# An integer mask for a sine's argument, and batch 1's first stage begun two units sooner in a fused Fourier-mixing and maxout kernel

## The chip, the core and the metric

The kernel runs on one core of one Trainium2 chip. The metric is the device time of one execution in microseconds (us). Five queues matter: TensorE (PE, with its weight loads as PEld), VectorE (DVE), ScalarE (ACT), GpSimd (POOL, which also issues the loads of x and the scattered stores) and SyncE (SP, which only issues DMAs). Each works its instructions off in the order of the program.

## The reference

```python
def _attn_ref(x):                      # x: (8, 3072, 256)
    X = np.fft.fft(x, axis=1)
    X = np.fft.fft(X, axis=2)
    return X.real.astype(np.float32)

def _moe_ref(x, w1, w2, w3, w_out):    # x: (24576, 256), w: (256, 768), w_out: (768, 256)
    h = np.maximum(np.maximum(x @ w1, x @ w2), x @ w3)
    return h @ w_out
```

The output of the first, as 24576 rows of 256, is the input of the second.

## The kernel before

The Fourier transform along the 256 columns is folded into the weights: `md_all` and `nmd_all` hold a sine and its negative, of 256 columns each in two halves, and `product` multiplies them with the weights into `g_all` and, by `differ`, `gd_all`. The transform along the 3072 rows is made for each of the 8 batches by class `Mix` in two stages. Stage one is the pieces `s0` to `s6`: each multiplies up to eight of the 49 slabs of `xt` (one of two buffers, by the batch's parity) with the small table `tab` into PSUM, and an eviction copies that to `tb` (L403, L406, L412, L414). Stage two is the pieces `k`: matmuls of `yb` with the tables `te_tab` and `to_tab` (L464), evicted to `tE` and `tO`. Between the stages `tb` must become `yb`, transposed: for batch 0 by one DVE transpose (`t`, L432), for later batches through DRAM, by pieces `y` (`tb` to `db`, L421) and `z` (`db` to `yb`, L427), four DMAs each, on the SP queue. Piece `x` (`x0`) then writes one more column into `yb` (L453, L454, on ACT), so it waits for all four DMAs of `z`. Before stage one the upper half of `xt` must be filled with a mirrored copy of the lower (`mirror`, L134 and L138: on DVE for batch 0, on POOL or DVE for batch 1, on ACT afterwards).

The main loop has 18 units a batch (3 blocks of 512 tokens by 6 chunks of 128 hidden columns), 144 in all. A unit makes `pse` tiles on PE (`begin`; L488, L489, or L831, L832 for a split unit), and ACT and DVE take the maximum into `hp` (`unit_out`: ACT `stmp`, L501, then DVE, L502); then the unit before is finished with `gd_all` (`finish`, L495) and taken into `hm`. From unit 7 on every odd unit is split: the third weight goes ahead through `third` (PE L815 and L817, ACT `odd` L819, DVE `even` L820, POOL `plus` and `minus` L824), and DVE alone takes the maximum (L833, L845). Below, hp6 is the `hp` of unit 6, hm5 the `hm` of unit 5. The finished block is multiplied with `wout_bf` (L511, `l2_block`) over the following units, evicted by DVE (`ot`, L539), and stored by SP (L547) and POOL (L620).

What else is done in a unit is a plan by hand: `at(b, u, fn)`. The units 0 to 5 of batch 0 carry the rest of the preparation: `column` (psc, L354), `prep_second` (psw, L377, evicted to `gw` by DVE, L382, then ACT, L383). `ahead0` says which pieces of batch 1 go in which unit of batch 0:

```python
ahead0 = {5: ("s0", "s1"), 6: ("s2", "y0", "s3"), 7: ("s4", "s5", "s6", "y1", "u"),
          8: ("z0", "z1"), 12: ("x",), 13: ("kO0",), 14: ("v0", "kE0", "kO1"), ...
```

The pieces `s`, `k`, `e3`, `d3`, `pl`, `psc` and `psw` share the three PSUM banks of pool `ps_f`.

In the prologue (up to some 20 us) x of batch 0 comes in four chunks (`FIRST`), c0 to c3, of two loads each. DVE's order there is: small tables, `vm` (the argument of `md_all`'s sine), mirror c0, the reduction of `vm` by `_reduce` (L23, L25, L27), `wrap(0, 512)`, mirror c1, `wrap(512, 1024)`, mirror c2, mirror c3, three small ones for `sgn`, the eviction of s5 and the transpose. Matmuls named `warm` (L638) only keep PE busy.

Of the kernel before, what the change touches and what calls it, by code (L numbers as in the profile page):

```python
# [9 lines left out]
FP32 = mybir.dt.float32  # L10
BF16 = mybir.dt.bfloat16
INT32 = mybir.dt.int32
UINT32 = mybir.dt.uint32
AX = mybir.ActivationFunctionType
ALU = mybir.AluOpType
# [5 lines left out]
def _reduce(nc, w, v, q, period):  # L21

    nc.vector.tensor_scalar(out=q, in0=v, scalar1=1.0 / period, scalar2=ROUND,  # L23
                            op0=ALU.mult, op1=ALU.add)
    nc.vector.tensor_scalar(out=q, in0=q, scalar1=-ROUND, scalar2=-period,  # L25
                            op0=ALU.add, op1=ALU.mult)
    nc.vector.tensor_tensor(out=w, in0=v, in1=q, op=ALU.add)  # L27
# [24 lines left out]
def kernel(  # L52
# [9 lines left out]
    nc = tc.nc  # L62
# [38 lines left out]
    md_all = consts.tile([128, 512], BF16, tag="md_all")  # L101
    nmd_all = consts.tile([128, 512], BF16, tag="nmd_all")
# [26 lines left out]
    def mirror(b, s0, s1):  # L129

        t = xt[b % 2]
        fn = (nc.vector.tensor_copy, (nc.gpsimd.tensor_copy, nc.vector.tensor_copy)[s0 >= 25],
              nc.scalar.copy)[min(b, 2)]
        fn(out=t[64:128, s0:s1, 1:128], in_=t[0:64, s0:s1, 255:128:-1])  # L134
        if b < 2:
            if b == 0 and s0 < 40:
                fn = nc.scalar.copy
            fn(out=t[64:128, s0:s1, 0], in_=t[0:64, s0:s1, 128])  # L138
# [6 lines left out]
    gen = ctx.enter_context(tc.tile_pool(name="gen", bufs=1))  # L145
# [20 lines left out]
    kvec = gen.tile([128, NHALF + 1], FP32, tag="kvec")  # L166
# [38 lines left out]
    ang_o = gen.tile([128, NA], FP32, tag="ang_o")  # L205
    nc.vector.memset(ang_o, 0.0)
    rnd = gen.tile([128, 2], FP32, tag="rnd")
    nc.vector.memset(rnd[:, 0:1], ROUND)
    nc.vector.memset(rnd[:, 1:2], -ROUND)
    nc.vector.memset(ang_o[:, 15:32], 8.0)  # L210
# [2 lines left out]
    def small(name):  # L213
        return gen.tile([128, 1], FP32, name=name, tag=name)

    def scal(out, in0, s1, op0, s2=None, op1=None, eng=None):
        kw = {} if op1 is None else {"op1": op1}
        return (eng or nc.vector).tensor_scalar(out=out, in0=in0, scalar1=s1, scalar2=s2,
                                                op0=op0, **kw)

    def mad(out, in0, s1, in1):
        return nc.vector.scalar_tensor_tensor(out=out, in0=in0, scalar=s1, in1=in1,
                                              op0=ALU.mult, op1=ALU.add)
# [6 lines left out]
    phi, s_of = small("phi"), small("s_of")  # L230
# [8 lines left out]
    ang_q = gen.tile([128, NA], FP32, tag="ang_q")  # L239
    mad(ang_r, ang_r, alpha, ang_o)  # L240
    _reduce(nc, ang_r, ang_r, ang_q, 32.0)
    nc.scalar.activation(out=ang_q, in_=ang_r, func=AX.Sin, scale=float(2.0 * math.pi / 32.0))
    par = gen.tile([128, 2], FP32, tag="par")
    odd = gen.tile([128, 1], INT32, tag="odd")
    nc.vector.tensor_scalar(out=odd, in0=pidx_i, scalar1=1, scalar2=None, op0=ALU.bitwise_and)
    scal(par[:, 1:2], odd, 64.0, ALU.mult)
    scal(par[:, 0:1], odd, -64.0, ALU.mult, 64.0, ALU.add)
    nc.vector.tensor_copy(out=tab[:, 0:64:2], in_=ang_q[:, 0:32])
    scal(tab[:, 1:64:2], ang_q[:, 0:32], sig, ALU.mult)
    scal(tabx, ang_q[:, 32:NA], sgm, ALU.mult)  # L250

    dve = nc.vector.tensor_copy
    vm = gen.tile([128, 512], FP32, tag="vm")
    qm = gen.tile([128, 512], FP32, tag="qm")
    pf = gen.tile([128, 2], FP32, tag="pf")
    for fc in range(2):
        scal(pf[:, fc:fc + 1], pidx, float(128 * fc), ALU.add)
        for k, c in ((0, 64.0), (1, 0.0)):
            scal(vm[:, (2 * fc + k) * 128:(2 * fc + k + 1) * 128], dvec, pf[:, fc:fc + 1], ALU.mult,
                 c, ALU.add)  # L260

    q = gen.tile([128, NHALF + 1], FP32, tag="q")
    step = float(2.0 * math.pi / 3072.0)

    def phase(c0, c1):
        nc.scalar.activation(out=kvec[:, c0:c1], in_=kvec[:, c0:c1], func=AX.Identity,
                             scale=s_of, bias=phi)

    def turns(c0, c1):

        nc.scalar.activation(out=q[:, c0:c1], in_=kvec[:, c0:c1], func=AX.Identity,
                             scale=1.0 / 3072.0, bias=rnd[:, 0:1])
        nc.scalar.activation(out=q[:, c0:c1], in_=q[:, c0:c1], func=AX.Identity,
                             scale=1.0, bias=rnd[:, 1:2])

    def wrap(c0, c1):
        mad(kvec[:, c0:c1], q[:, c0:c1], -3072.0, kvec[:, c0:c1])

    phase(0, 512)
    turns(0, 512)  # L280
    phase(512, 1024)
    mirror(0, *FIRST[0])
    turns(512, 1024)
    _reduce(nc, vm, vm, qm, 256.0)
    nc.vector.tensor_copy(out=vm.rearrange("p (fc k c) -> p fc k c", fc=2, k=2)[:, :, :, 0],
                          in_=par.unsqueeze(1).to_broadcast([128, 2, 2]))
    wrap(0, 512)
# [360 lines left out]
    mirror(0, *FIRST[2])  # L648
    m.s(2, pool=ps_s)
    m.s(3, pool=ps_s)  # L650
    nc.scalar.activation(out=md_all, in_=vm, func=AX.Sin, scale=float(2.0 * math.pi / 256.0))
    warm_up(1)
    mirror(0, *FIRST[3])
    m.s(4, pool=ps_s)
# [2 lines left out]
    scal(sgn, sgn, 2.0, ALU.mult, -1.0, ALU.add)  # L657
    scal(dif, sgn, 1.0, ALU.subtract)
    m.s(5, pool=ps_s, evict=dve)
    m.s(6, pool=ps_s)  # L660
    m.t()
    warm_up(2)
    nc.scalar.activation(out=nmd_all, in_=vm, func=AX.Sin, scale=float(-2.0 * math.pi / 256.0))
    for k in range(3):
        load_w(k, 384, 768)
    m.u()
# [1 line left out]
    for (s0, s1) in HALVES:  # L668
        for h in range(2):
            load_x(1, s0, s1, h)  # L670
        if s0 == 0:
            nc.gpsimd.dma_start(out=wout_bf.rearrange("p (jc c) -> p jc c", jc=NJC),
                                in_=moe_w_out.rearrange("(jc p) c -> p jc c", jc=NJC))
# [59 lines left out]
    def at(b, unit, fn):  # L733
        plan.setdefault((b + unit // UNITS, unit % UNITS), []).append(fn)

    def piece(b, what):
        mm = mix(b)
        if what[0] == "s":
            mm.s(int(what[1:]), evict=dve if b == 1 and what in ("s3", "s5") else nc.scalar.copy)
        elif what[0] == "y":  # L740
            mm.y(*((0, 24), (24, NS))[int(what[1])])
        elif what[0] == "z":
            mm.z(int(what[1]))
        elif what[0] == "u":
# [12 lines left out]

    def fetch(b, k):
        half, h = divmod(k, 2)
        load_x(b, *HALVES[half], h)  # L760
# [14 lines left out]
        at(0, u, fn)  # L775

    for ch in range(4):
        at(0, (3, 3, 5, 5)[ch], lambda ch=ch: mirror(1, *CHUNKS[ch]))
        at(0, 4, lambda ch=ch: fetch(2, ch))
    for b in range(2, B):  # L780
        for ch in range(4):
# [2 lines left out]
        for ch in range(8):  # L784
            at(b - 2, 5 + ch + 3 * (b == 2), lambda b=b, ch=ch: turn(b, ch))
        at(b - 2, 13 + 3 * (b == 2), lambda b=b: mirror_first(b))

    ahead0 = {5: ("s0", "s1"), 6: ("s2", "y0", "s3"), 7: ("s4", "s5", "s6", "y1", "u"),
              8: ("z0", "z1"), 12: ("x",), 13: ("kO0",), 14: ("v0", "kE0", "kO1"),
              15: ("v1", "kE1"), 16: ("kO2",), 17: ("v2", "kE2", "end")}  # L790
    ahead = {1: ("s0", "s1"), 2: ("s2", "y0", "s3", "s6"), 3: ("s4", "s5", "y1", "u"),
             6: ("z0",), 7: ("z1",), 11: ("x",), 12: ("kO0",), 13: ("v0", "kE0", "kO1"),
# [1 line left out]
    for b in range(B - 1):  # L794
        for u, whats in (ahead0, ahead)[min(b, 1)].items():
            for what in whats:
                at(b, u, lambda b=b, what=what: piece(b + 1, what))
# [123 lines left out]
```

## Time and profile before

| what | value |
|---|---|
| median of 3 runs | 396.98 us (396.65 to 397.41) |
| profiled execution, its own time | 397.9 us |
| its span on the core | 396.1 us |
| PE, DVE, ACT, POOL busy | 96%, 80%, 67%, 84% of the span |
| q1 (DMAs of SP): packets, MB | 41978, 26.72 |
| q0 (DMAs of POOL): packets, MB | 24368, 26.53 |

The median and the profiled execution are executions of the same program; the span leaves out what lies before the first and behind the last instruction, 1.8 us here. Times in the rows of the profile count from the start of the span. In a row of the timeline the brackets say how long the engine had been idle before the instruction, and what ended that.

### The profile page before, as it was taken

What the parts mean: (1) busy time and instruction counts of PE and PEld (TensorE: products, weight loads), DVE (VectorE), ACT (ScalarE), POOL (GpSimd) and SP (SyncE); (2) the same over time, 40 slices, a digit from 0 to 9 for tenths busy, and PEclk for the clock granted to TensorE, in tenths of its full rate; (3) what the DMA queues carried; (4) which work ended last, traced back from release to release, by engine and by line L of the source; (5) the groups of instructions that cost most, each with busy time, mean ns of one, the idle gap of its engine ahead of it and who ended that gap; (6) DMA issues with size and microseconds to landing.
All of it is one profiled execution on the core that took longest, in us unless ns stands there. A gap on an engine that the chain in (4) does not pass through costs nothing.

```text
span 396.1 us, 8431 instructions
## 1 busy us (share of the span) xinstructions
PE 380.5 (96%) x2759; PEld 235.8 (60%) x2759; DVE 316.5 (80%) x528; ACT 263.7 (67%) x478; POOL 332.0 (84%) x432
## 2 busy tenths in 40 slices
PE   6699999999999999999999999999999999999994
PEld 2355555665665666656665666656665666666673
DVE  7986877787887988877887887877887887887982
ACT  5877669578867787578866788568866547545420
POOL 9994687879988899889988899889977898869993
PEclk9999999999999999999999999999999999999998
DMA  8999576494656876595666867395343553421234
GB/s 114 181 182 162 117 190 126 114 211 132 137 153 117 199 150 153 121 207 129 136 155 112 203 139 167 109 207 130 117 103 93 140 142 93 91 84 45 89 94 132
DMA packets 66901, 54.20 MB, mean 137 GB/s; under 512 B 32702, under 2 KB 62556, under 8 KB 66003
## 3 DMA queue, kind: packets, MB, share of 16 engines
q0 software_dynamic: 24368, 26.53, 35.2%
q1 hardware_dynamic: 41978, 26.72, 27.5%
q8 instruction: 21, 0.34, 0.4%
q10 hardware_dynamic: 512, 0.43, 0.4%
q14 instruction: 22, 0.18, 0.2%
HBM read 36.95 MB, written 30.81 MB: 171 GB/s over the span
## 4 chain that ended last, share of the span: by engine, by line
PE 88%; DMA 4%; DVE 2%; ACT 2%; POOL 1%; issue 1%; DVEq 0%; POOLq 0%; SPq 0%
PE po L511 30%; PE pse L495 12%; PE pse L488 8%; PE pse L489 8%; PE po L534 5%; PE pse L831 4%; PE pse L832 4%; PE e L815 4%; PE d L817 4%; PE ps L399 3%; PE ps L464 3%; PE pl L526 2%; DMA yb<-db 2%; DMA xt<-in_x_dram 2%; DVE yb L432 1%
## 5 line engine op out<-in xcount | busy, mean ns | idle before, releaser
L501 ACT ACTIVATE stmp<-pse 128x512 bf16<-128x512 f32 x150 | 89.5, 601 | 65.1 <-PE pse L495 41.4
L824 POOL TENSOR_TENSOR plus<-even,odd 128x512 bf16<-128x512 f32 x69 | 87.7, 1272 | 36.3 <-DVE even L820 28.5
L620 POOL DMA_INDIRECT out_dram<-ot,rows_m x92 | 102.4, 1113 | 17.9 <-issue 8.6
L824 POOL TENSOR_TENSOR minus<-even,odd 128x512 bf16<-128x512 f32 x69 | 87.5, 1268 | 0.0
L511 PE MATMUL po<-wout_bf,hp 128*128 128x256 bf16 x576 | 86.1, 273 | 0.0
L833 DVE SCALAR_TENSOR_TENSOR hp<-pse,plus 128x512 bf16<-128x512 f32 x69 | 47.6, 689 | 46.6 <-PE pse L832 27.1
L511 PE MATMUL po<-wout_bf,hm 128*128 128x256 bf16 x576 | 78.6, 273 | 0.0
L511 PEld LDWEIGHTS <-hp 128*128 128x128 bf16 x576 | 56.3, 98 | 26.1
L495 PE MATMUL pse<-tO,gd_all 128*128 128x512 bf16 x219 | 70.8, 379 | 0.0
L511 PEld LDWEIGHTS <-hm 128*128 128x128 bf16 x576 | 56.3, 98 | 16.4
L539 DVE TENSOR_TENSOR ot<-po,even 128x512 f32<-128x512 f32 x92 | 62.7, 681 | 0.0
L502 DVE TENSOR_TENSOR hm<-pse,stmp 128x512 bf16<-128x512 f32 x75 | 51.6, 688 | 9.4 <-ACT stmp L501 6.2
L502 DVE TENSOR_TENSOR hp<-pse,stmp 128x512 bf16<-128x512 f32 x75 | 51.3, 684 | 9.3 <-ACT stmp L501 8.0
L488 PE MATMUL pse<-tE,g_all 128*128 128x512 bf16 x150 | 56.8, 379 | 1.5 <-ACT stmp L501 0.7
L489 PE MATMUL pse<-tO,g_all 128*128 128x512 bf16 x150 | 56.8, 379 | 0.0
L820 DVE SCALAR_TENSOR_TENSOR even<-vb,wcol,e 128x512 f32<-128x512 bf16 x69 | 50.9, 737 | 0.0
L845 DVE SCALAR_TENSOR_TENSOR hm<-pse,minus 128x512 bf16<-128x512 f32 x69 | 47.0, 681 | 1.0 <-PE pse L489 0.5
L819 ACT ACTIVATE odd<-d 128x512 f32<-128x512 f32 x69 | 41.3, 599 | 6.0
L134 ACT COPY xt<-xt 64x762 bf16<-64x762 bf16 (+1 forms) x48 | 40.3, 839 | 1.1
L495 PEld LDWEIGHTS <-gd_all 128*128 128x128 bf16 x219 | 21.3, 97 | 23.0 <-issue 5.0
L534 PE MATMUL po<-gw,tO 128*128 128x512 bf16 x92 | 34.9, 380 | 0.0
L403 ACT CAST tb<-ps 128x512 bf16<-128x512 f32 x40 | 21.6, 588 | 14.8 <-PE ps L399 14.8
(175 smaller groups left out, 482.9 us busy)
## 6 DMA issues: line engine op xcount, KB each, us to landing
xt<-in_x_dram POOLq DMA_DIRECT2D x14, 384.0 KB, 8.7
out_dram<-ot SPq DMA_DIRECT2D x55, 96.0 KB
out_dram<-ot SPq DMA_DIRECT2D x64, 64.0 KB
db<-tb SPq DMA_DIRECT2D x21, 192.0 KB
vb<-vd SPq DMA_DIRECT2D x23, 128.0 KB
xt<-in_x_dram POOLq DMA_DIRECT2D x7, 400.0 KB, 6.7
xt<-in_x_dram POOLq DMA_DIRECT2D x7, 368.0 KB, 11.6
out_dram<-ot SPq DMA_DIRECT2D x62, 32.0 KB
```

Source lines behind the costliest of these rows:

```text
L488: nc.tensor.matmul(pse[:, 0:n], g_all[:, jc, 2 * i, :], te, start=True, stop=False)
L489: nc.tensor.matmul(pse[:, 0:n], g_all[:, jc, 2 * i + 1, :], to, start=False, stop=True)
L495: nc.tensor.matmul(pse, gd_all[:, jc, i, :], to, start=False, stop=True, skip_group_check=True)
L501: nc.scalar.activation(out=stmp[:, 0:n], in_=pses[0][:, 0:n], func=AX.Relu)
L502: nc.vector.tensor_tensor(out=dst, in0=src3, in1=stmp[:, 0:n], op=ALU.max)
L511: nc.tensor.matmul(po, hcols(jc), wout_bf[:, jc * 256:(jc + 1) * 256], start=False, stop=(jc == NJC - 1), skip_group_check=True)
L534: nc.tensor.matmul(po, to[:, cp], gw[:, 256:768], start=True, stop=True)
L539: nc.vector.tensor_tensor(out=ot.rearrange("p (h c) -> p h c", h=2), in0=po.rearrange("p (h c) -> p h c", h=2), in1=lin.unsqueeze(1).to_br ...
L620: stored(nc.gpsimd.indirect_dma_start(out, bass.IndirectOffsetOnAxis(ap=rows_m[0:128 - lo, at_row: at_row + 1], axis=0), ot[lo:128, 256:51 ...
L820: nc.vector.scalar_tensor_tensor(out=even3, in0=vb, scalar=wcol[:, jc:jc + 1], in1=e3, op0=ALU.mult, op1=ALU.add)
L824: nc.gpsimd.tensor_tensor(out=dst, in0=even3, in1=odd3, op=op)
L833: nc.vector.scalar_tensor_tensor(out=dst, in0=pse2, scalar=0.0, in1=sums[g][0], op0=ALU.max, op1=ALU.max)
```

## The change

The argument of the sine in `md_all` becomes an integer: `vm` and `par` are INT32 and offset by 128, one `bitwise_and` with 255 takes the place of the three operations of `_reduce`, and the two sines get a bias of minus and plus pi (`turn`). On ACT `phase(0, 512)` stands ahead of the small sine, and the sine to `md_all` stands behind the eviction of s4 and no longer ahead of it. Of batch 1, s0 and s1 go from unit 5 to 3, s2 and y0 from 6 to 4, s3 and s4 to 5, s5, s6, y1 and `u` to 6, z0 and z1 from 8 to 7; the mirrors on DVE of its second half go from unit 5 to 4. Its evictions s0, s1, s2 and s4 are on DVE (before: s3 and s5), the others on ACT. Later batches and the units from 8 on are as before.

```diff
+    turn = gen.tile([128, 2], FP32, tag="turn")
+    nc.vector.memset(turn[:, 0:1], -math.pi)
+    nc.vector.memset(turn[:, 1:2], math.pi)
...
+    def phase(c0, c1):
+        nc.scalar.activation(out=kvec[:, c0:c1], in_=kvec[:, c0:c1], func=AX.Identity,
+                             scale=s_of, bias=phi)
+
+    phase(0, 512)
     nc.scalar.activation(out=ang_q, in_=ang_r, func=AX.Sin, scale=float(2.0 * math.pi / 32.0))
-    par = gen.tile([128, 2], FP32, tag="par")
+    par = gen.tile([128, 2], INT32, tag="par")
...
-    scal(par[:, 1:2], odd, 64.0, ALU.mult)
-    scal(par[:, 0:1], odd, -64.0, ALU.mult, 64.0, ALU.add)
+    scal(par[:, 1:2], odd, 64.0, ALU.mult, 128.0, ALU.add)
+    scal(par[:, 0:1], odd, -64.0, ALU.mult, 192.0, ALU.add)
...
-    vm = gen.tile([128, 512], FP32, tag="vm")
-    qm = gen.tile([128, 512], FP32, tag="qm")
+    vm = gen.tile([128, 512], INT32, tag="vm")
...
-        for k, c in ((0, 64.0), (1, 0.0)):
+        for k, c in ((0, 192.0), (1, 128.0)):
...
-    phase(0, 512)
     turns(0, 512)
...
-    _reduce(nc, vm, vm, qm, 256.0)
+    nc.vector.tensor_scalar(out=vm, in0=vm, scalar1=255, scalar2=None, op0=ALU.bitwise_and)
...
-    nc.scalar.activation(out=md_all, in_=vm, func=AX.Sin, scale=float(2.0 * math.pi / 256.0))
     warm_up(1)
     mirror(0, *FIRST[3])
     m.s(4, pool=ps_s)
...
     m.s(5, pool=ps_s, evict=dve)
+    nc.scalar.activation(out=md_all, in_=vm, func=AX.Sin, scale=float(2.0 * math.pi / 256.0),
+                         bias=turn[:, 0:1])
     m.s(6, pool=ps_s)
     m.t()
     warm_up(2)
-    nc.scalar.activation(out=nmd_all, in_=vm, func=AX.Sin, scale=float(-2.0 * math.pi / 256.0))
+    nc.scalar.activation(out=nmd_all, in_=vm, func=AX.Sin, scale=float(-2.0 * math.pi / 256.0),
+                         bias=turn[:, 1:2])
...
-            mm.s(int(what[1:]), evict=dve if b == 1 and what in ("s3", "s5") else nc.scalar.copy)
+            mm.s(int(what[1:]), evict=dve if b == 1 and what in ("s0", "s1", "s2", "s4") else nc.scalar.copy)
...
-        at(0, (3, 3, 5, 5)[ch], lambda ch=ch: mirror(1, *CHUNKS[ch]))
+        at(0, (3, 3, 4, 4)[ch], lambda ch=ch: mirror(1, *CHUNKS[ch]))
...
-    ahead0 = {5: ("s0", "s1"), 6: ("s2", "y0", "s3"), 7: ("s4", "s5", "s6", "y1", "u"),
-              8: ("z0", "z1"), 12: ("x",), 13: ("kO0",), 14: ("v0", "kE0", "kO1"),
+    ahead0 = {3: ("s0", "s1"), 4: ("s2", "y0"), 5: ("s3", "s4"), 6: ("s5", "s6", "y1", "u"),
+              7: ("z0", "z1"), 12: ("x",), 13: ("kO0",), 14: ("v0", "kE0", "kO1"),
```

More of the change, by code (lines that the diff above doesn't have):

```diff
@@ L263 @@
     step = float(2.0 * math.pi / 3072.0)
-    def phase(c0, c1):
-        nc.scalar.activation(out=kvec[:, c0:c1], in_=kvec[:, c0:c1], func=AX.Identity,
-                             scale=s_of, bias=phi)
     def turns(c0, c1):
```

## The prediction

> **What bounds the kernel now.** I read the page first, then stretches of the span, then the chain of work that ended last, then the timelines of the stretches where PE idles. A change of 0.2% (0.8 us) is about what a measurement here can tell from none.
>
> ```profile
> PE 380.5 (96%) x2759; PEld 235.8 (60%) x2759; DVE 316.5 (80%) x528; ACT 263.7 (67%) x478; POOL 332.0 (84%) x432
> ```
>
> In the rows of the stretches stand the length, then busy us (and instructions) of PE, PEld, DVE, ACT and POOL, then PE's granted clock, the share of the DMA engines and GB/s.
>
> ```profile
> 20.00:37.35 17.35, 15.95 (x144) 9.30 (x141) 13.18 (x22) 13.21 (x30) 13.39 (x28) 1.00 1.11 172
> 37.35:45.36 8.01, 7.25 (x44) 3.71 (x43) 6.45 (x13) 5.88 (x12) 2.78 (x3) 1.00 0.72 132
> 45.36:59.83 14.47, 13.66 (x92) 8.59 (x91) 10.91 (x18) 9.81 (x18) 12.41 (x17) 1.00 0.68 166
> 59.83:65.00 5.17, 4.92 (x42) 3.00 (x43) 3.83 (x6) 5.07 (x9) 3.98 (x5) 1.00 0.87 150
> 65.00:380.00 315.00, 315.00 (x2280) 196.57 (x2279) 257.38 (x404) 214.37 (x383) 272.12 (x327) 1.00 0.58 133
> ```
>
> From 65 to 380 us PE is never idle at full clock: nothing in those 315 us can be gained, and what PE gains ahead of them reaches the end whole. The idle PE is 17.35-15.95 = 1.40, 0.76, 0.81 and 0.25 us in the four stretches ahead, 3.22 us together, and the prologue ahead of 20 us, which hangs on a chain and not on PE. The change works only there.
>
> ```profile
> 5.35 6.28 DMA xt<-in_x_dram
> ...
> 15.23 0.70 DVE tb L406
> 16.04 3.76 DVE yb L432
> ...
> 59.53 0.07 ACT yb L453
> ```
>
> The chain runs through the eviction of s5 into the transpose, and late in batch 0 it leaves PE for ACT's L453, which waits for `yb` from DRAM.
>
> **Part 1, the prologue.** DVE in order, then PE's s5 and the last load of chunk c3 (its issue, and 6.3 us to landing):
>
> ```profile
> 8.88 0.43 DVE L23 TENSOR_SCALAR qm<-vm 128x512 f32<-128x512 f32 x1
> 9.35 0.86 DVE L25 TENSOR_SCALAR qm<-qm 128x512 f32<-128x512 f32 x1
> 10.24 0.69 DVE L27 TENSOR_TENSOR vm<-vm,qm 128x512 f32<-128x512 f32 x1
> ...
> 11.78 0.77 DVE L134 COPY xt<-xt 64x2032 bf16<-64x2032 bf16 x1
> 12.58 0.69 DVE L222 SCALAR_TENSOR_TENSOR kvec<-q,kvec 128x512 f32<-128x512 f32 x1
> 13.30 0.92 DVE L134 COPY xt<-xt 64x1016 bf16<-64x1016 bf16 x2
> 14.15 0.24 DVE L138 COPY xt<-xt 64x9 bf16<-64x9 bf16 x1
> ```
>
> ```profile
> 14.78 0.41 PE L399 MATMUL ps<-xt,tab 128*64 128x512 bf16 x2
> 6.99 0.61 POOL L127 DMA_DIRECT2D xt<-in_x_dram  x1
> xt<-in_x_dram POOLq DMA_DIRECT2D x1, 128.0 KB, 6.3
> ```
>
> DVE has no gap from 8.88 to the end of c3's mirror: it sets when s2 to s5 can go. The three operations of the reduction take 8.88 to 10.93, 2.05 us. The mask is an operation of the form of L23 or L25 on integers, which the trace does not show; those two rows bound it, 0.43 to 0.86, and I take 0.43; the landing of c3, below, decides either way. That frees 1.6 us (1.2 at the other end). The two memsets of `turn` and the small sine behind `phase` (0.2 us later, so `tab` also) cost DVE some 0.2 us of it. Not all arrives: c2's last load lands at 5.35 + 6.28 = 11.63, early enough for a c2 mirror near 12.0, but c3's lands at 6.99 + 6.3 = 13.3. So DVE waits there, whatever the mask costs: mirror c3 from 13.35 (now 13.30 + 0.92/2 = 13.76), L138 done at 14.03 and not 14.39. What is late next is PE: s5 runs at 14.78 behind s4 and two warm matmuls, and s4 waits for c2's mirror. With that mirror over a microsecond sooner (now done at 13.76), s4 and its warm matmuls are over well ahead of c3's, and s5 runs at 14.1. Then the eviction of s5 starts at 14.6 (now 15.23), and the transpose follows: **0.6 us** gained. On ACT `md_all` now stands behind s4's eviction; with s4 over a microsecond sooner than s5 there is room for it ahead of s6, and PE needs it only behind s6. Bounds: 0.65, set by the landing, and 0.3, should ACT's work in units 0 to 2 take part of it back.
>
> **Part 2, units 3 to 9.** Times here are those of the trace, without the 0.6.
>
> ```profile
> 31.18 0.38 PE L488 MATMUL pse<-tE,g_all 128*128 128x512 bf16 x1 [0.68 <-ACT stmp L501]
> 33.50 0.38 PE L488 MATMUL pse<-tE,g_all 128*128 128x512 bf16 x1
> 40.59 0.89 PE L399 MATMUL ps<-xt,tab 128*64 128x512 bf16 x4 [0.23 <-ACT odd L819]
> 43.90 0.62 PE L399 MATMUL ps<-xt,tab 128*64 128x512 bf16 x4
> 44.99 0.22 PE L409 MATMUL ps<-xt,tab 128*64 128x128 bf16 x1 [0.46 <-ACT tb L403]
> 47.31 0.38 PE L831 MATMUL pse<-tE,g_all 128*128 128x512 bf16 x1
> ```
>
> ```profile
> 33.35 0.58 ACT L466 CAST tO<-ps 128x512 bf16<-128x512 f32 x1
> 37.63 0.47 ACT L383 ACTIVATE gw<-psw,sgn 128x256 bf16<-128x256 f32 x1 [1.89 <-DVE gw L382]
> 38.00 1.06 ACT L403 CAST tb<-ps 128x512 bf16<-128x512 f32 x2
> ```
>
> ```profile
> 32.95 0.69 DVE L502 TENSOR_TENSOR hp<-pse,stmp 128x512 bf16<-128x512 f32 x1 [1.00 <-ACT stmp L501]
> 36.91 0.69 DVE L382 CAST gw<-psw 128x512 bf16<-128x512 f32 x1 [0.60 <-PE psw L377]
> 42.98 0.69 DVE L833 SCALAR_TENSOR_TENSOR hp<-pse,plus 128x512 bf16<-128x512 f32 x1 [0.77 <-POOL plus L824]
> 45.45 0.68 DVE L403 CAST tb<-ps 128x512 bf16<-128x512 f32 x1
> 46.04 0.68 DVE L845 SCALAR_TENSOR_TENSOR hm<-pse,minus 128x512 bf16<-128x512 f32 x1
> ```
>
> Two pieces `s` are four matmuls, 0.62 us in the row of 43.90, some 0.55 without the overlap with what follows; the 0.89 of 40.59 has a wait of 0.27 inside. s0 and s1 now stand just ahead of PE's wait of 0.68 at 31.18: they cost nothing there. Their two DVE copies (0.6 each from start to start, as 45.45 to 46.04) fit into DVE's idle 1.00 ahead of 32.95, and put hp4 off by some 0.2. s2 is dearer: it stands ahead of PE's 33.50 and takes the PSUM bank that ACT's copy of 33.35 frees at 33.93, 0.4 later, and adds half of 0.55 itself. psc and psw, and with them DVE's `gw`, come 0.7 later than 36.91, and ACT's `gw`, which waits for it, too. DVE's mirrors and s2's copy fill the time ahead of that `gw` and push hp5 and hm4 back by over a microsecond, which nothing on PE needs before unit 6's second bank. Behind ACT's `gw` stands one copy to `tb` and not two (0.53 less), so hp6, even7, POOL's plus7 and hp7 (42.98) come 0.2 to 0.3 later. From there on things go the other way. On PE the waits of 0.23, 0.27 and 0.46 at the banks are gone and 0.55 of work lies in what was idle, against the new 0.4: 1.1 ahead. The DVE copy at 45.45 is gone too, so hm7 starts at 46.04 + 0.3 - 0.6 = 45.75 and frees unit 9's bank at 46.45, where PE begins unit 9 at 47.31 now. The later of the two decides: about **0.75 us** gained. Bounds: 1.1 (PE alone) and 0 (DVE's chain 0.75 later still).
>
> **Part 3, the way through DRAM.**
>
> ```profile
> 45.56 0.85 SPq L547 DMA_DIRECT2D out_dram<-ot  x2
> 49.55 1.69 SPq L427 DMA_DIRECT2D yb<-db  x4
> ```
>
> ```profile
> 59.53 0.23 ACT L453 CAST yb<-psx 128x16 bf16<-128x16 f32 x1 [2.34 <-DMA out_dram<-ot]
> 59.83 0.39 PE L464 MATMUL ps<-to_tab,yb 128*128 128x96 bf16 x6 [0.81 <-ACT yb L454]
> ```
>
> The row names a store, but L453 waits for the four DMAs of `z`; the last lands 59.5-49.55 = 9.9 us after the first is issued. ACT idles 2.34 us, PE 0.81 behind it, and 0.25 more up to 65 while ACT catches up. After the change s5 and s6 stand at PE's 40.59 and leave ACT near 42 (0.53 a copy from start to start), y1 goes at once, and z stands behind the first two stores, which end at 45.56 + 0.85 = 46.4: 3.1 us sooner. What is late next: L453 is itself some 1.4 us sooner by parts 1 and 2, at 55.8, and z, at the same 9.9, lands near 56. What is left of ACT's wait is under 0.5, and PE has 2.34-0.81 = 1.5 of slack to it. So **1.0 us** of the 1.06 goes; 0.5 at the other end, if z is slower. On SP, y0 now stands ahead of a load to `vb` for block 2, which is needed only from unit 11.
>
> The Trainium skill, "DMA: Bandwidth & Descriptors", section "Anatomy of one DMA", fits 2.0 us plus bytes over 436 GB/s, which would be an estimated 3.8 us for z's 784 KB (49 rows of 16 KB), and by it L453 would not have waited at all; the trace has 9.9. Its section on queues says that a DMA engine takes turns between queues, by which z would land sooner the less it overlaps the loads of x, and part 3 would be 1.06 and not 1.0. I keep the row.
>
> **The sum.** 0.6 + 0.75 + 1.0 = 2.35 us. On the profiled execution that is 396.1 to 393.75 in the span (397.9 to 395.55 in its own time); from the median of the runs, 396.98 - 2.35 = **394.6 us**.
>
> **Rivals.**
> - DVE eats part 2. For it: hp5, hm4 and `gw` stand behind five more DVE instructions. Against: DVE idles 1.00 and 0.60 there. Then 0.6 + 1.0 = 1.6 gained: 395.4. Chance 0.14.
> - z lands late all the same, with half of part 3 lost and part 2 cut to 0.3: 0.6 + 0.3 + 0.5 = 1.4, 395.6. Chance 0.06.
> - Other waits take the place of most: ACT, 5.07 busy of 5.17 at 59.83, and POOL set the pace after all, and no more than 0.5 is left: 396.5. Chance 0.10.
> - Slower: DVE stands still in unit 4. Its mirrors, now ahead of s2's copy, hp5, hm4 and `gw`, need the second half of batch 1's x:
>
> ```profile
> 18.24 1.29 POOL L127 DMA_DIRECT2D xt<-in_x_dram  x2
> 25.50 1.55 POOL L134 COPY xt<-xt 64x1651 bf16<-64x1651 bf16 x1 [0.31 <-DMA xt<-in_x_dram]
> ```
>
>  The first half landed at 25.5; wout and the second half stand behind it, 1136 KB (384, and 23.5 slabs of 32 KB by each of its two loads), an estimated 6.6 us at the stretch's 172 GB/s, so 32.0, against DVE's arrival at 33.7 (32.95 + 0.2, two steps of 0.6 for hp4 and hm3, less part 1). If it landed as late as DVE's present use of it, right behind `gw` at 37.6, the stall would be 3.9 us and pass by `gw` to unit 9: 3.9 - 2.35, and a little of part 3 back, +1.4: 398.4. It is slower than no change from a landing at 36.1 on. Chance 0.08.
>
> **Numbers.** Forecast 0.62. Its own range is gains of 0.8 (0.3 + 0 + 0.5) to 2.8 (0.65 + 1.1 + 1.06), 394.2 to 396.2. With the rivals at 395.4 and 395.6 inside and 0.3 either way, about the runs' own spread around their median, the range is 393.8 to 396.5. Faster by over 0.2%: 0.62 + 0.14 + 0.06 = 0.82; within 0.2%: 0.10; slower: 0.08.
>
> **What would show it.** Right: the transpose (L432) starts near 15.4; PE's wait of 0.68 in unit 3 has matmuls of batch 1 in its place; z is issued near 45.8 (0.6 sooner than the 46.4 above); L453 waits under 0.5 us and PE's wait of 0.81 ahead of stage two is gone; idle PE between 20 and 65 us falls from 3.2 to about 1.5. Wrong: a transpose still near 16; idle time on DVE in front of its mirrors in unit 4; PE waiting over 0.5 us for hp7 or hm7; L453 still waiting over 1.5 us; or idle PE past 65.

## The result, and the profile after

The changed kernel takes **395.00 us** (median of 7 runs, 394.68 to 395.99) against 396.65 (396.32 to 397.41) of the kernel before in runs on the same chip: a ratio of 0.9960, with a 95% interval of 0.9948 to 0.9973, or 1.6 us less (1.1 to 2.1). The prediction said 394.6, in 393.8 to 396.5, and faster at 0.82. The profiled execution took 395.75, its span 393.8 (before: 397.9 and 396.1), so the spans of the two profiles differ by 2.3. Executions whose mean granted clock is 0.994 or less are longer than others of the same kernel: of 29 runs of before on one chip 7 are such, with a median span of 396.0, and the 22 others have 394.9.

Line numbers behind the edit are shifted: L399, L403, L406, L432, L453, L464 and L831 of before are L401, L405, L408, L434, L455, L466 and L835.

First the prologue, in DVE's timeline of the changed kernel (start, us, engine, line, operation; in brackets the idle time ahead and what ended it).

```profile
8.88 0.43 DVE L286 TENSOR_SCALAR vm<-vm 128x512 int32<-128x512 int32 x1
...
10.76 0.69 DVE L134 COPY xt<-xt 64x2032 bf16<-64x2032 bf16 x1 [0.64 <-DMA xt<-in_x_dram]
...
12.21 0.42 DVE L134 COPY xt<-xt 64x1016 bf16<-64x1016 bf16 x1
13.57 0.49 DVE L134 COPY xt<-xt 64x1143 bf16<-64x1143 bf16 x1 [0.95 <-DMA xt<-in_x_dram]
13.98 0.17 DVE L138 COPY xt<-xt 64x9 bf16<-64x9 bf16 x1
...
14.66 0.69 DVE L408 CAST tb<-ps 128x512 bf16<-128x512 f32 x1
15.46 3.77 DVE L434 STREAM_TRANSPOSE yb<-tb 128x2048 uint32<-128x2048 uint32 x1
```

One mask of 0.43 stands where three operations stood. DVE now waits for x: 0.64 at c1 and 0.95 at c3, whose load is issued at 6.97 and lands 6.52 later, at 13.49. The transpose starts 1.97 behind that, at 15.46 and not 16.04.

The stretches of the prediction, in the changed kernel (length, then busy us and instructions of PE, PEld, DVE, ACT, POOL):

```profile
20.00:37.35 17.35, 15.88 (x136) 9.21 (x137) 14.71 (x29) 13.33 (x29) 14.38 (x29) 1.00 1.20 190
37.35:45.36 8.01, 7.96 (x50) 4.37 (x48) 5.65 (x10) 5.80 (x12) 3.31 (x5) 1.00 0.88 167
45.36:59.83 14.47, 14.25 (x100) 9.20 (x100) 13.22 (x21) 12.21 (x21) 13.22 (x17) 1.00 0.64 154
59.83:65.00 5.17, 5.12 (x48) 3.46 (x47) 3.37 (x6) 4.84 (x9) 4.67 (x6) 1.00 0.73 157
```

Idle PE in them is 1.47, 0.05, 0.22 and 0.05: 1.8 us where it was 3.2, and 1.5 was said. Some 50 of PE's records are missing from this trace (2710 on PE, 2759 on PEld in the page's first line), so a little of that is no wait. In PE's and DVE's timelines:

```profile
33.43 0.41 PE L401 MATMUL ps<-xt,tab 128*64 128x512 bf16 x2 [0.40 <-ACT tO L468]
...
45.98 0.38 PE L835 MATMUL pse<-tE,g_all 128*128 128x512 bf16 x1
...
57.52 0.39 PE L466 MATMUL ps<-to_tab,yb 128*128 128x96 bf16 x6
```

```profile
42.78 0.69 DVE L837 SCALAR_TENSOR_TENSOR hp<-pse,plus 128x512 bf16<-128x512 f32 x1 [1.45 <-POOL plus L828]
...
45.25 0.68 DVE L849 SCALAR_TENSOR_TENSOR hm<-pse,minus 128x512 bf16<-128x512 f32 x1
```

The wait of 0.68 in unit 3 is filled with s0 and s1; s2 waits 0.40 for its bank; unit 9 begins at 45.98 (before 47.31), just as hm7 ends on DVE (45.25 + 0.68); stage two of batch 1 begins at 57.52 (before 59.83) and waits for nothing. In SP's and ACT's timelines z is issued 3.2 sooner and L455 no longer waits:

```profile
45.35 0.84 SPq L549 DMA_DIRECT2D out_dram<-ot  x2
46.31 1.41 SPq L429 DMA_DIRECT2D yb<-db  x4
...
55.87 0.23 ACT L455 CAST yb<-psx 128x16 bf16<-128x16 f32 x1
```

### The profile page after: what moved, and what is told of

Same layout as the page of the kernel before. It is cut to its first block, busy times and chain, and to the rows that moved or that the text cites. A ratio compares the mean times of both kernels' runs of the same rounds, so it can differ in the third digit from the quotient of the medians.

```text
span 393.8 us, 8383 instructions
## 1 busy us (share of the span) xinstructions
PE 377.7 (96%) x2710; PEld 235.9 (60%) x2759; DVE 315.0 (80%) x530; ACT 263.0 (67%) x476; POOL 332.9 (85%) x432
## 4 chain that ended last, share of the span: by engine, by line
PE 84%; DMA 4%; DVE 4%; ACT 3%; issue 2%; POOL 2%; SPq 1%; DVEq 0%; ACTq 0%; POOLq 0%
PE po L513 30%; PE pse L497 12%; PE pse L490 8%; PE pse L491 7%; PE po L536 4%; PE d L821 4%; PE pse L835 4%; PE e L819 3%; PE ps L466 3%; PE pse L836 3%; PE pl L528 2%; PE ps L401 2%; DMA yb<-db 2%; DMA xt<-in_x_dram 2%; ACT tb L405 1%
## 5 line engine op out<-in xcount | busy, mean ns | idle before, releaser
L490 PE MATMUL pse<-tE,g_all 128*128 128x512 bf16 x148 | 56.0, 379 | 1.9 <-DVE tE L468 0.5
L491 PE MATMUL pse<-tO,g_all 128*128 128x512 bf16 x131 | 49.6, 379 | 0.2 <-issue 0.2
L536 PE MATMUL po<-gw,tO 128*128 128x512 bf16 x85 | 32.3, 380 | 0.0
L405 ACT CAST tb<-ps 128x512 bf16<-128x512 f32 x38 | 20.5, 588 | 14.1 <-PE ps L401 14.1
```

Source lines behind the costliest of these rows:

```text
L490: nc.tensor.matmul(pse[:, 0:n], g_all[:, jc, 2 * i, :], te, start=True, stop=False)
L491: nc.tensor.matmul(pse[:, 0:n], g_all[:, jc, 2 * i + 1, :], to, start=False, stop=True)
L536: nc.tensor.matmul(po, to[:, cp], gw[:, 256:768], start=True, stop=True)
```

## Reading all profiles by four marks

The experiments below gave more profiles than their times could tell apart, as kernels with the new prologue start their transpose up to 0.8 us apart from run to run. Four starts on the timelines divide the way into pieces: the transpose, unit 9 on PE, stage two of batch 1 on PE (its first row of matmuls of `yb`, L464 or L466), and unit 19 (L831 or L835). "Ratio" is the one to the kernel before on the same chip, with its 95% interval; in the first row the median is that of the runs beside the changed kernel.

| kernel | transpose | unit 9, and behind the transpose | z issued | stage two | unit 19, and behind unit 9 | median us | ratio |
|---|---|---|---|---|---|---|---|
| before | 16.04 | 47.31, 31.27 | 49.55 | 59.83 | 73.31, 26.00 | 396.65 | 1 |
| before_again | 15.88 | 47.16, 31.28 | 49.41 | 58.71 | 72.07, 24.91 | 397.14 | 1.0004 [0.9990, 1.0017] |
| prologue_alone | 15.17 | 46.46, 31.29 | 48.70 | 58.00 | 71.31, 24.85 | 396.33 | 0.9988 [0.9979, 0.9998] |
| schedule_alone | 15.49 | 45.99, 30.50 | 46.32 | 57.53 | 70.30, 24.31 | 395.48 | 0.9963 [0.9949, 0.9976] |
| changed | 15.46 | 45.98, 30.52 | 46.31 | 57.52 | 70.29, 24.31 | 395.00 | 0.9960 [0.9948, 0.9973] |
| mask_old_order | 15.57 | 46.06, 30.49 | 46.39 | 57.60 | 70.37, 24.31 | 395.04 | 0.9949 [0.9936, 0.9961] |
| z_unit8 | 15.03 | 45.54, 30.51 | 45.87 | 57.08 | 69.86, 24.32 | 395.38 | 0.9958 [0.9945, 0.9971] |
| y1_unit7 | 14.94 | 45.45, 30.51 | 48.77 | 58.30 | 71.79, 26.34 | 397.02 | 1.0000 [0.9989, 1.0010] |
| old_evict | 15.58 | 47.00, 31.42 | 47.33 | 58.53 | 71.31, 24.31 | 395.78 | 0.9963 [0.9949, 0.9978] |
| mirrors_unit5 | 15.47 | 47.48, 32.01 | 47.81 | 59.02 | 71.80, 24.32 | 396.63 | 0.9993 [0.9980, 1.0006] |
| s2_unit5 | 15.63 | 46.07, 30.44 | 46.40 | 57.61 | 70.38, 24.31 | 395.21 | 0.9954 [0.9936, 0.9971] |
| x_late | 15.75 | 49.36, 33.61 | 49.69 | 60.90 | 73.67, 24.31 | 397.42 | 1.0004 [0.9991, 1.0017] |
| prologue_tail | 15.54 | 47.77, 32.23 | 48.10 | 59.31 | 72.08, 24.31 | 395.89 | 0.9978 [0.9963, 0.9993] |
| best | 15.89 | 46.90, 31.01 | 47.23 | 58.44 | 71.21, 24.31 | 395.84 | 0.9968 [0.9955, 0.9982] |

The first distance is part 2, and repeats to 0.03 (31.27 to 31.29 with the old plan, 30.49 to 30.52 with the new). The second is part 3: 24.31 or 24.32 wherever L455 does not wait for z, and more where it does. The transpose is part 1, and moves with the loads of x. Rows of the last mark, in PE's timelines of before, of before_again and of the changed kernel:

```profile
73.31 0.38 PE L831 MATMUL pse<-tE,g_all 128*128 128x512 bf16 x1
```

```profile
72.07 0.38 PE L831 MATMUL pse<-tE,g_all 128*128 128x512 bf16 x1
```

```profile
70.29 0.38 PE L835 MATMUL pse<-tE,g_all 128*128 128x512 bf16 x1
```

Between the two first profiles the changed kernel is 3.02 ahead at unit 19: 0.58 by the transpose, 0.75 up to unit 9 and 1.69 behind it. Against before_again it is 1.78: 0.42, 0.76 and 0.60. The two profiles of before are 1.24 apart there and 1.2 in their spans. From unit 19 to the end of the span it is 322.7 to 322.9 us in twelve of the fourteen profiles, 323.4 in schedule_alone and 323.5 in the changed kernel.

## The experiments

**Each half alone.** `prologue_alone` is the kernel before with the mask and ACT's new order; `schedule_alone` is the kernel before with the new plan.

```diff
 # prologue_alone, against the changed kernel
-evict=dve if b == 1 and what in ("s0", "s1", "s2", "s4") else ...
+evict=dve if b == 1 and what in ("s3", "s5") else ...
-at(0, (3, 3, 4, 4)[ch], lambda ch=ch: mirror(1, *CHUNKS[ch]))
+at(0, (3, 3, 5, 5)[ch], lambda ch=ch: mirror(1, *CHUNKS[ch]))
 ... ahead0 as before
```

> The kernel before with the prologue's part alone (the mask, the phase ahead of the small sine, md_all behind s5's matmuls); batch 1's pieces, mirrors and evictions stand as before. By the prediction's steps part 1 is worth 0.6 us and reaches the end whole: the transpose at L434 starts at 15.4 to 15.5 (16.04 before) and the span is 0.6 shorter, 395.5 and 396.4 by time (ratio 0.9985). Rival: the shift of the prologue is eaten on the way (ACT or POOL late in units 0 to 2, x of batch 1 issued later): the transpose is as early, but stage one's last unit, unit 9, still starts at 47.3 and the time does not move (ratio 1.000). A second rival: the prologue alone carries most of the 1.65 us, because its shift lets z's DMAs and the banks meet otherwise: ratio 0.997.

Measured: 0.9988, 0.5 us (0.1 to 0.8). The shift of the transpose arrives at unit 9 whole, 31.29 behind it as in before: not eaten. Its profile shows something else in ACT's and PE's timelines:

```profile
57.52 0.23 ACT L455 CAST yb<-psx 128x16 bf16<-128x16 f32 x1 [1.19 <-DMA yb<-db]
...
58.00 0.39 PE L466 MATMUL ps<-to_tab,yb 128*128 128x96 bf16 x6
```

z is issued 8.82 before L455 and not 9.98 as in the first profile of before; ACT waits 1.19 and PE not at all.

> The kernel before with batch 1's schedule alone (pieces in units 3 to 7, mirrors in 3 and 4, DVE evicting s0, s1, s2, s4); the prologue keeps the reduction. By the prediction's steps parts 2 and 3 remain: 0.75 + 1.0 = 1.75 us, a span of 394.4 (ratio 0.9956). The transpose stays at 16.0, unit 9 starts at 46.5 to 46.6 (47.31 before, 45.98 with both), z is issued near 46.9 (49.55 before) and stage two of batch 1 on PE starts near 58.1 (59.83 before, 57.52 with both). Rival, the parts do not add: the schedule needs the 0.6 of the prologue to have its mirrors or banks free in time, unit 9 stays at 47.0 or later, and the gain is under 1.0 (ratio 0.9975 or more).

Measured: 0.9963, 1.5 us (1.0 to 2.0). Unit 9 is 30.50 behind the transpose, so the plan needs nothing from the prologue. But the transpose is at 15.49 with the old reduction. In DVE's timeline of schedule_alone:

```profile
9.36 0.43 DVE L25 TENSOR_SCALAR qm<-qm 128x512 f32<-128x512 f32 x1
...
13.58 0.49 DVE L134 COPY xt<-xt 64x1143 bf16<-64x1143 bf16 x1 [0.32 <-DMA xt<-in_x_dram]
...
15.49 3.75 DVE L432 STREAM_TRANSPOSE yb<-tb 128x2048 uint32<-128x2048 uint32 x1
```

The reduction's second operation took 0.43, and 0.86 in the first profile of before; with that DVE is ready for c3 0.32 before it lands, and the mask could bring nothing here.

**The profile of before again**, the kernel unchanged.

> The kernel before, unchanged, with a profile of its own. The four profiles taken so far, two of them of kernels with one and the same prologue, have the transpose at 15.03 to 15.57 where the first profile of before has 16.04, and the span of that profile, 396.1, lies 1.0 above the median span of 17 later runs (395.1). Theory now: that profile was a dear one of its kind, and the terms of the prediction's sum were sized on it. Then this profile has a span of 394.5 to 395.6, the reduction's second operation (L25) at 0.43 and not 0.86, c3's mirror waiting for its load or at most 0.3 behind it, the transpose at 15.2 to 15.7, and L453 waiting about 1.2 to 2.0 us in place of 2.34, so that PE waits 0 to 0.5 ahead of stage two and not 0.81. Rival: the first profile is typical in these places (0.86, 16.04, 2.34, 0.81 within 0.15 each) and the span differs elsewhere.

Its DVE rows, and its rows on ACT and PE:

```profile
9.34 0.71 DVE L25 TENSOR_SCALAR qm<-qm 128x512 f32<-128x512 f32 x1
...
15.88 3.76 DVE L432 STREAM_TRANSPOSE yb<-tb 128x2048 uint32<-128x2048 uint32 x1
```

```profile
58.29 0.23 ACT L453 CAST yb<-psx 128x16 bf16<-128x16 f32 x1 [1.25 <-DMA yb<-db]
...
58.71 0.39 PE L464 MATMUL ps<-to_tab,yb 128*128 128x96 bf16 x6
```

Half of it as theory said: the span is 394.9, L453 waits 1.25, PE not at all. The prologue is nearer to the first profile (0.71, 15.88). So the 2.34 and the 0.81 on which part 3 was sized belong to one execution: z landed 9.98 behind its issue there, 8.88 here, 8.82 in prologue_alone, 9.23 in y1_unit7.

**ACT's order in the prologue**: phase and md_all at their old places, the mask kept.

```diff
-    phase(0, 512)
     nc.scalar.activation(out=ang_q, ...)
 ...
     m.s(3, pool=ps_s)
+    nc.scalar.activation(out=md_all, in_=vm, func=AX.Sin, ..., bias=turn[:, 0:1])
     warm_up(1)
```

> The changed kernel with ACT's old order in the prologue: the phase behind the small sine, md_all behind s3 and not behind s5's matmuls; the mask stays. By the prediction the order on ACT is no term of the 0.6: DVE's chain up to c3's landing sets it, so the transpose stays at 15.4 to 15.5 and the time at 395.0 (ratio to the kernel before 0.9955 to 0.9965). Rival: the old place of md_all, 0.74 us and now waiting for the mask, stands ahead of s4's eviction on ACT and holds s4 and with it s5 or s6: the transpose starts at 15.8 to 16.2 and 0.3 to 0.6 of the gain is lost.

```profile
13.69 0.73 ACT L653 ACTIVATE md_all<-vm,turn 128x512 bf16<-128x512 int32 x1
14.31 0.59 ACT L408 CAST tb<-ps 128x512 bf16<-128x512 f32 x1
```

Measured: 0.9949, and a transpose 2.03 behind c3's landing (1.97 in the changed kernel). In ACT's timeline md_all stands ahead of s4's eviction and ends in time; the order on ACT is no term.

**z in unit 8.**

```diff
-              7: ("z0", "z1"), 12: ("x",), ...
+              8: ("z0", "z1"), 12: ("x",), ...
```

> The changed kernel with one thing put back: z0 and z1 in unit 8 and not 7. By part 3 this gives back most of 1.0 us: z is issued at 48 to 49 (46.31 in the changed kernel), at the same 9 to 10 us it lands at 57.5 to 58.5, L455 (due at 55.87) waits 1.7 to 2.7 us, PE's slack of 1.5 to it is used up and PE idles 0.2 to 1.1 ahead of stage two: span 0.2 to 1.1 longer than the changed kernel's, most likely 0.7 (394.5; ratio to the kernel before 0.9975). Rival: z, issued later, lands sooner after its issue, as DMA queues are freer then (6 to 8 us): no wait on PE and the time of the changed kernel (ratio 0.996).

Both theories missed: z is 30.84 behind the transpose, as in the changed kernel (30.85). SP's order is the same in the two programs, since no store is added between the two places; SP waits for the first two stores in both. The run is a repeat of the changed kernel, 0.9958, with a transpose 0.43 sooner and a landing of c3 0.45 sooner. Not z's unit brings z forward, but what stands ahead of it.

**y1 in unit 7, z in 8**, with everything else new.

```diff
-6: ("s5", "s6", "y1", "u"), 7: ("z0", "z1"), 12: ...
+6: ("s5", "s6"), 7: ("y1", "u"), 8: ("z0", "z1"), 12: ...
```

> The changed kernel with y1 and u in unit 7 and z in unit 8, as before, so that on SP y1 stands behind the first two stores again and z behind y1's landing (z alone in unit 8 left SP's order as it is). Part 3's price by itself: y1 issued at 46.2, z at about 49.2 (46.31 in the changed kernel); with a landing 8.8 to 9.9 us after its issue, at 58.0 to 59.1, L455, due at 55.87, waits 2.1 to 3.2 us, PE's slack of 1.5 is used up, and PE waits 0.6 to 1.7 ahead of stage two: 0.6 to 1.7 us longer than the changed kernel, about 396.0 (ratio to the kernel before 0.9975). Rival: z then lands within 8 us of its issue and costs PE under 0.3 (ratio 0.996).

```profile
48.77 1.62 SPq L429 DMA_DIRECT2D yb<-db  x4
...
58.00 0.23 ACT L455 CAST yb<-psx 128x16 bf16<-128x16 f32 x1 [2.69 <-DMA out_dram<-ot]
...
58.30 0.39 PE L466 MATMUL ps<-to_tab,yb 128*128 128x96 bf16 x6 [1.16 <-ACT yb L456]
```

Measured: 1.0000. With y1 behind the stores z starts 3.0 later against unit 9 (3.32 behind it and not 0.33), ACT waits 2.69, PE 1.16, and unit 19 is 2.03 later. The waits are as expected; the loss is over the 0.6 to 1.7 that was said, as PE's wait of 1.16 is not all of it. All that parts 1 and 2 bring is gone.

**Which engine evicts**: s3 and s5 on DVE, as before.

```diff
-evict=dve if b == 1 and what in ("s0", "s1", "s2", "s4") else nc.scalar.copy
+evict=dve if b == 1 and what in ("s3", "s5") else nc.scalar.copy
```

> The changed kernel with DVE evicting s3 and s5 of batch 1 as before, and ACT all others. By part 2's reading DVE's copies fit into its idle time in unit 3, while ACT's copies of s0, s1 and s2 would stand in its queue between the stmp of units 3 and 4, and s5's copy on DVE behind hm6: hp4 and hp5 come 1.0 or more later, unit 9 at 46.3 to 46.8 (45.98 in the changed kernel), y1 and z later by 0.5 to 1: 0.3 to 0.8 us longer than the changed kernel (ratio to the kernel before 0.9975). Rival: the split between the two engines is no term, only the units of the pieces are: time of the changed kernel (ratio 0.996).

```profile
33.46 0.69 DVE L504 TENSOR_TENSOR hp<-pse,stmp 128x512 bf16<-128x512 f32 x1 [1.97 <-ACT stmp L503]
...
34.45 0.41 PE L401 MATMUL ps<-xt,tab 128*64 128x512 bf16 x2 [1.27 <-ACT tO L468]
```

ACT's copies of s0 and s1 put its `stmp` off, DVE waits 1.97 for it, s2 waits 1.27 for its bank, and unit 9 is 31.42 behind the transpose: all of part 2 is gone in the profile, and unit 9 starts at 47.00, later than the 46.3 to 46.8 that was said. By its ratio, 0.9963, the loss does not show within the intervals. The granted clock makes it plainer: in the executions above 0.994 the median span is 393.85 here (6 runs), 393.1 in the changed kernel (7, in another set of runs) and 394.9 in before (22 beside this run; 394.9 and 395.0 in two other sets). So some 0.75 us are lost, near the 0.9 of the mark; the rest of the gain stays, as z is in time (24.31).

**Where the last two mirrors stand**: unit 5, as before.

```diff
-        at(0, (3, 3, 4, 4)[ch], ...)
+        at(0, (3, 3, 5, 5)[ch], ...)
```

> The changed kernel with the last two mirrors of batch 1 in unit 5, as before, where they stand ahead of s3's and s4's matmuls. If the mirrors' place is no term (the prediction gave it none by itself), 30.5 us from the transpose to unit 9 again and 395.0 (ratio 0.996). Rival: the mirrors, behind DVE's gw, hold s4 on PE (s4 needs slabs of the last two chunks): DVE's two copies of 0.55 and two of 0.19 put s4 0.5 to 1.3 later, and unit 9 0.4 to 1.0 later: 395.4 to 396.0 (0.9975).

```profile
38.63 0.96 PE L401 MATMUL ps<-xt,tab 128*64 128x512 bf16 x4 [1.48 <-DVE xt L138]
```

The rival held, and by more than it said (0.4 to 1.0 later): s3 and s4 wait 1.48 on PE for the mirrors, unit 9 is 1.5 later (32.01), and the time is that of the kernel before.

**s2 in unit 5**, to be rid of its wait of 0.40.

```diff
-4: ("s2", "y0"), 5: ("s3", "s4"), 6: ...
+5: ("s2", "y0", "s3", "s4"), 6: ...
```

> The changed kernel with s2 and y0 in unit 5 and not 4. From the start of the transpose to the start of unit 9 on PE it is 31.27 to 31.29 us in the three profiles with batch 1's old schedule and 30.49 to 30.52 in the five with the new one and DVE's new evictions. PE's wait of 0.40 at s2 for the bank of ACT's copy to tO should go, and gw come 0.7 sooner; by that 30.1, and 0.4 us off the end (394.6; ratio to the kernel before 0.995). Rival: DVE's hm7, which frees unit 9's bank just as PE comes, holds it, or three s in unit 5 wait for banks as long as s2 did in unit 4: 30.5 and 395.0 (0.996).

```profile
37.76 0.41 PE L401 MATMUL ps<-xt,tab 128*64 128x512 bf16 x2 [0.73 <-ACT gw L385]
```

The 0.40 is gone and a wait of 0.73 behind ACT's `gw` has come in unit 5: 30.44, nothing won that the time could show (0.9954). That is the second half of the rival.

**The second half of x late.** Its two loads stand in unit 4 on POOL.

```diff
-    for (s0, s1) in HALVES:                # batch 1, both halves, in the prologue
+    # in the prologue the first half only
+    for h in range(2):
+        at(0, 4, lambda h=h: load_x(1, 25, NS, h))
```

> The changed kernel with the two loads of the second half of batch 1's x issued on POOL in unit 4, behind its mirrors of the first half, at about 29.2 and not 18.8. It puts a price on the prediction's slower rival, DVE standing still at its mirrors in unit 4: a landing at 35 to 36.5 against DVE's arrival at 33.8 is a stall of 1.2 to 2.7 us, which by that rival passes through gw to unit 9 and to the end one to one, with z later by as much: 1.2 to 2.7 us longer than the changed kernel, about 397.0 (ratio to the kernel before 1.000). The other theory: POOL, DVE and ACT take most of it back by unit 9, 0.5 us or less is left (ratio 0.997).

```profile
33.47 0.68 DVE L504 TENSOR_TENSOR hm<-pse,stmp 128x512 bf16<-128x512 f32 x1
37.27 0.55 DVE L134 COPY xt<-xt 64x1524 bf16<-64x1524 bf16 x1 [3.12 <-DMA xt<-in_x_dram]
```

DVE stands still for 3.12 (x lands at 37.2), and unit 9 is 33.61 behind the transpose, 3.09 more: one to one. The time is that of the kernel before (1.0004), as expected.

**A shorter way from c3 to the transpose, and both ideas together.** `best` has s2 in unit 5 beside the edit below.

```diff
-            if b == 0 and s0 < 40:
+            if b == 0:                     # L138 of c3 on ACT
 ...                                        # s5: slabs 40 to 43 by DVE, 44 to 47 by ACT
-    m.s(5, pool=ps_s, evict=dve)
-    nc.scalar.activation(out=md_all, ...)
-    m.s(6, pool=ps_s)
+    m.s(5, pool=ps_s, evict=(dve, nc.scalar.copy))
+    m.s(6, pool=ps_s, evict=dve)
     m.t()
+    nc.scalar.activation(out=md_all, ...)
```

> The changed kernel with a shorter chain from the landing of c3 to the transpose: the copy of c3's first columns (L138) on ACT and not behind the mirror on DVE, s5's eviction split between DVE and ACT (half of 0.69 each), s6's eviction on DVE, md_all behind s6. In five profiles with the mask the transpose starts 1.97 to 2.06 after c3's landing; here 0.2 less by L138 and 0.3 less by the split: 1.5 to 1.6. The transpose's absolute start lies with the landing (13.0 to 13.8 so far). 0.4 to 0.5 us off the end: 394.55 (ratio 0.995). Rival: md_all and nmd_all, 0.5 later, and s5's half on ACT hold the products of unit 0, so stage two does not start sooner: 395.0 (0.996).

> s2 in unit 5 and the shorter chain of the prologue together. If both theories hold, 0.8 to 0.9 off the changed kernel: 394.2 (ratio to the kernel before 0.9935), transpose 1.5 to 1.6 behind c3's landing and unit 9 30.1 behind the transpose. If neither does, 395.0 (0.996).

In ACT's and PE's timelines of prologue_tail:

```profile
15.09 0.37 ACT L410 CAST tb<-ps 128x256 bf16<-128x256 f32 x1 [0.67 <-DVE tb L410]
...
16.14 0.39 PE L313 MATMUL psg<-w_bf,md_all 128*128 128x128 bf16 x2 [0.98 <-ACT md_all L665]
```

Both theories failed, and the rival of the first held in its step (stage two no sooner) but not in its time (395.0 said, 395.89 measured). ACT's half of s5 waited for DVE's half (0.67), so the two ran one behind the other and the transpose is 2.03 behind the landing, no sooner; why the one waits for the other was not tried. md_all behind that is late, and PE waits 0.98 for it. In `best` the same 0.98 stands and unit 9 is 31.01 behind the transpose; in prologue_tail it is 32.23 behind, and the 1.22 between them is not that wait. Here are the 4 us behind it in prologue_tail and in best (as in the stretches above, the granted clock is the third number from the end):

```profile
16.00:20.00 4.00, 3.64 (x28) 2.97 (x29) 3.24 (x1) 2.42 (x6) 3.96 (x9) 0.57 1.26 178
```

```profile
16.00:20.00 4.00, 3.19 (x38) 2.72 (x39) 3.63 (x1) 3.48 (x9) 4.00 (x8) 1.00 1.09 150
```

In prologue_tail PE was granted 0.57 of its clock there, and the products ahead of `psx` (L313) take 3.6 us where best needs 2.3. So the 32.23 is in good part that of one execution. Among executions with a granted clock above 0.994, which its profile is not, prologue_tail has a median span of 393.7 (9 runs) and best 393.9 (10), 0.6 and 0.8 over the changed kernel's 393.1. No version is measurably faster than the changed kernel.

## Why the prediction was right, and where not

The time came within 0.4 of the forecast, and part of that is luck: 2.35 us less were forecast and 1.65 were measured by the medians, 0.7 too much, and 0.33 of that is hidden because the forecast starts from 396.98, the median of three runs, and the seven runs give 396.65.

**Part 1, 0.6.** The step held: the mask took the 0.43 that was chosen, c3's landing sets the mirror, ACT's order plays no part, and the shift reaches unit 9 whole. The size was one execution's: the transpose is 16.04, 15.88 and 15.49 with the reduction, 14.94 to 15.75 in the nine profiles with the mask and the old way to the transpose. It is 0 where the reduction is done before c3 lands, and 0.5 us (0.1 to 0.8) by the runs.

**Part 2, 0.75.** Right, and in its steps: 31.27 to 30.52 is 0.75. s2 waited its 0.40, hp7 came 0.4 later (said 0.2 to 0.3) and hm7 at 45.25, 45.83 without the shift, where 45.75 was said. What the prediction gave no price by itself is what carries it: with the mirrors in unit 5 or the old evictions there is nothing left of it (32.01 and 31.42). The rival "DVE eats part 2" did not come about.

**Part 3, 1.0.** Right in kind, z soon enough and no wait at L455, and mis-sized twice. (z itself came at 46.31 and not near 45.8: the two stores ahead of it are issued at 45.35, 0.2 sooner than before and not 0.6, and L455 had room for that.) First, it was read from an execution with a late z; in before_again PE has no wait at that place. Second, more than the idle rows goes by a late z. The prediction counted 0.81 and 0.25 up to 65; by starts it is 1.69 in that profile: 0.98 up to stage two (59.83, against 47.31 and the 11.54 that the changed kernel takes from unit 9) and 0.71 behind it. In before_again it is 0.60, all behind it, though PE shows no wait. The stretch from stage two to its fourth row of `yb` matmuls, in before_again and the changed kernel:

```profile
58.71:64.56 5.85, 5.69 (x51) 3.62 (x48) 4.44 (x7) 5.75 (x11) 5.13 (x7) 1.00 0.84 162
```

```profile
57.52:62.77 5.25, 5.20 (x49) 3.63 (x48) 3.85 (x7) 4.92 (x9) 4.78 (x6) 1.00 0.87 157
```

The same work takes 0.60 longer, but PE's busy time grows by 0.49 of that. Two rows of each, in PE's timelines, show why:

```profile
59.38 0.38 PE L489 MATMUL pse<-tO,g_all 128*128 128x512 bf16 x1
59.80 0.38 PE L488 MATMUL pse<-tE,g_all 128*128 128x512 bf16 x1
```

```profile
58.19 0.38 PE L491 MATMUL pse<-tO,g_all 128*128 128x512 bf16 x1
58.40 0.38 PE L490 MATMUL pse<-tE,g_all 128*128 128x512 bf16 x1
```

A matmul is busy 0.38 in the rows, and the next starts 0.21 behind its start; here it starts 0.42 behind, 0.21 are lost, and 0.04 are to be seen as idle. That ACT, late by z and busy for 5.75 of the 5.85, hands this on is argued from its share; the rows do not name what each start waited for. So the step that failed is the reading of idle PE as all that can be gained: ahead of 65 it was 0.6 too little (1.69 against 1.06), and y1_unit7 shows the same (2.03 lost from unit 9 to unit 19, 1.40 of it idle). The prediction's 315 us without idle time behind 65, in which nothing was to be gained, rest on that reading too. On z's landing the fit of the Trainium skill, "DMA: Bandwidth & Descriptors", "Anatomy of one DMA", gave an estimated 3.8 us; the page has that fit for one DMA that GpSimd issues, and z is four that SP issues; 8.8 to 10.0 were measured in the four profiles that show it, so the row was the one to keep.

**The sum, 2.35.** The spans of the two profiles differ by 2.3, and it is partly chance: 3.02 up to unit 19, and then 0.76 given back in the changed profile by 106 (a split unit starts there at 106.32, before at 108.58), where z of batch 2 was late in its turn (ACT's and PE's rows). schedule_alone, with the same plan, shows that with an ACT wait of 0.77, and mask_old_order, z_unit8 and s2_unit5 not at all:

```profile
99.88 0.23 ACT L455 CAST yb<-psx 128x16 bf16<-128x16 f32 x1 [1.43 <-DMA yb<-db]
...
103.70 0.39 PE L466 MATMUL ps<-to_tab,yb 128*128 128x64 bf16 x6 [0.18 <-ACT odd L823]
```

So two steps of the prediction did not hold in this profile: what PE gains ahead of 65 did not reach the end whole, and idle PE past 65, one of its signs of being wrong, was there.

Taken from the median, the 2.35 was too much: the first profile's span of 396.1 is 1.0 over the median span of 17 later runs (395.1). Against before_again the parts make 1.78, and the runs say 1.6. There lies most of the 0.7 that was forecast too much.

**The slower rival** has its step right (3.12 of stall, 3.09 at unit 9) and not its condition: in the changed kernel DVE did not wait at these mirrors. Its break-even, a landing at 36.1, stays open: the profile of x_late has one at 37.2 and a time of 398.37, but the median is 397.42, level with before. What was not among the rivals is that y1 behind the first two stores by itself undoes the gain (1.0000), as the mirrors in unit 5 do (0.9993).

## What to carry to other kernels

Size a term from the distance between two marks that repeats over profiles, not from the idle rows of one execution: take a second profile of the kernel before, and put the sum on the run that it was read from. When a chain (here DMA through DRAM) has a due time, an edit that brings the consumer forward can be worth nothing unless the chain comes forward too (y1_unit7); price the two together. And a wait taken out of a tight plan can turn up at the next bank: s2's 0.40 came back as 0.73 behind `gw`.

## What the runs showed of the hardware

- The same loads of x take different times in kernels with the same loads: c3's last landed 5.99 to 6.82 us behind its issue, and the transpose followed 1.97 to 2.07 behind the landing in the eight profiles of the mask and the old way to the transpose whose chain names it. That is the scatter of the first mark.
- The reduction's L25, one operation of the same shape, took 0.86, 0.71 and 0.43. In the first two an issue of POOL's DMA (L184) was under way when it began, and it ended 0.2 behind that issue's end; in the third that issue began behind it. But L23 took 0.43 beside an issue in all three, so the cause stays open. The Trainium skill, "Trainium Architecture — The Big Picture", section "What this means for kernel authors", has VectorE and GpSimd share a port pair of SBUF under an exclusive lock; L25 would agree with that, L23 does not show it.
- The sine on integers with a bias takes 0.74 where it took 0.64 on floats without one (ACT's rows, before and after). The Trainium skill, "ScalarE: Activation LUTs", section "What ACT_TABLE_LOAD costs", puts a bias by pointer at some 93 ns; the 0.10 agrees. The integers have no price that shows: a sine on floats with such a bias (third row, of the changed kernel) takes 0.74 as well.

```profile
14.01 0.64 ACT L651 ACTIVATE md_all<-vm 128x512 bf16<-128x512 f32 x1
```

```profile
13.87 0.74 ACT L661 ACTIVATE md_all<-vm,turn 128x512 bf16<-128x512 int32 x1
```

```profile
30.62 0.74 ACT L305 ACTIVATE to_tab<-q,half_pi 128x513 bf16<-128x513 f32 x1
```

- The granted clock of PE can fall in one execution and stay in another. In prologue_tail it was 0.50 from 16.5 to 19.5, behind 0.98 us without work on PE; in best, behind the same 0.98, it was 1.00, so the wait alone does not decide it. None of the other profiles shows the fall between 16 and 20, and no execution of before with a low mean clock was profiled, so whether its longer span comes about in this way is not shown.
